# Attention of three of four batches: fp32 products on 64x64 tiles, and transposes on TensorE

## The chip, the cores and the metric

One core of one Trainium2 chip runs the whole program. The metric is the device time of one execution in microseconds (us), median of three runs.

## What is computed

Block-causal attention over 4 batches, 8 heads, 576 positions and 64 features per head, then two feed-forward layers on 2304 tokens of 512 features: 2048 hidden features with softplus, then 1536 with a gated SiLU behind an RMS norm.

```python
scores = scale * np.matmul(q, k.transpose(0, 1, 3, 2))
mask = block_i >= block_j              # blocks of 64 positions
attn = np.exp(scores - max); attn = attn / (sum + 1e-09)
x = np.matmul(attn, v)                 # then tokens x (heads * features)
h = x @ w_in; g = softplus(h); x = g @ w_out
xn = rms_norm(x) * rms_g
out = (silu(xn @ w_gate) * (xn @ w_val)) @ w_out
```

## The kernel before

**Order.** Every piece of work is registered with `op` (L82), with an engine, an estimated duration, a key (the wished time), and the tiles that it reads and writes. `Plan.schedule` (L145) then plays the whole program through with these estimates: on each engine it takes, among what is ready, the piece with the lowest key. `emit` (L271) does so up to 12 times with keys moved towards the latest possible times, and issues the instructions in the order of the best plan. The order on each engine is therefore fixed when the program is built; on the chip, an engine that waits for one instruction holds all behind it. `aop2`/`op2` (L424, L427) give pieces a choice of engines, and `schedule` picks by estimated end, with durations times `WEIGHT` (L74). PSUM has eight banks; `Banks` objects (L417) cap how many of them each kind of work may hold: feed-forward results `R_h`, attention `R_a` (scores and value products), transposes `R_tp`, and four accumulators `R_yp`.

**Feed-forward.** Tokens go in six blocks of 384 (`BLK`). Weights and activations are split into a high and a low fp32r part, and each product is three passes (`PASSES`). `g1` (L818) makes 128 hidden features with 12 matmuls of 384 columns, `g2` (L840) adds them into four accumulators with 12 more. The first phase runs 9 such steps for each of the six blocks, and attention of block j+1 is spread between the steps of block j; the second phase finishes the first layer, the third does the second layer (`g34`, L917, `g5`, L939). These two follow when attention is over.

**Attention.** A unit is one batch, one third of the query positions (`g`, 192 positions) and one pair of heads (`p`). It has three tiles `ib` of 64 positions; with two heads that is 128 rows, against n = 64 (3 g + ib + 1) keys. q lies block-diagonally, so that one matmul over 128 partitions gives both heads. `s_tile` (L594) makes the scores, takes the maximum on VectorE (L627), the exponential with the row sums on ScalarE (L661), and 1/sum (L669, L670). n = 576 goes in two halves of 288, as a bank holds 512 columns.

For batch 0 (`whole(u)`, L495; the first 12 units) the products are plain fp32, one matmul each, which the chip runs as two records; `s_turn` (L695) scales the probabilities, `turn` (L711) transposes them on TensorE in pieces of 128 columns, up to four a bank, and copies them out; `pv_whole` (L727) multiplies with v, for each head a matmul of 64 output rows, the two heads beside each other.

For batches 1 to 3, `prep_q`, `prep_k` and `prep_v` (L532 to L579) split q and k into two fp32r parts and v into two fp16 parts, the latter after scaling by a maximum that a small matmul (L561) spreads over the partitions. The scores are three passes of fp32r. `s_split` (L672) writes the probabilities as two fp16 halves, high (L681 to L683) and low (L686), and one DMA for each unit transposes them (L693). `pv` (L755) multiplies with v in three fp16 passes.

All matmuls but the transposes are issued at L422 (`mm`). `attention` (L789) registers the tiles in order; the value product of a unit follows its last tile by `LAG_T` = 6 tiles.

Of the kernel before, what the change touches and what calls it, by code (L numbers as in the profile page):

```python
# [68 lines left out]
class Plan:  # L69
# [4 lines left out]
    WEIGHT = {"ACT": 1, "DVE": 1, "POOL": 1}  # L74
# [7 lines left out]
    def op(self, eng, dur, key, fn, reads=(), writes=(), done=0.0, nbytes=0, after=(), alt=(), cols=0.0, port=False):  # L82
# [13 lines left out]
        for c in list(reads) + list(writes):  # L96
            b = c[0] if isinstance(c, tuple) else c
            if isinstance(b, Buf):
                if b.first is None:
                    b.first = i  # L100
                    if isinstance(b.ring, Banks):
                        self.takes[i] = b
# [42 lines left out]
    def schedule(self, key):  # L145
# [31 lines left out]
        for b in self.takes.values():  # L177
            b.ring.free = [0.0] * b.ring.cap
            for u in b.users:
                bank_of.setdefault(u, []).append(b)  # L180
            bank_left[b] = [len(b.users), 0.0]

        def at(i):
            t = max(free[eng[i]], ready_at[i])
            if i in self.takes:
                t = max(t, min(bank_free), min(self.takes[i].ring.free, default=INF))
            return t

        for _ in range(n):
# [16 lines left out]
            if i in self.takes:  # L206
                b = self.takes[i]
# [88 lines left out]
def t_mm(n):  # L296
    return max(0.11, (n + 32) / 2400)
# [46 lines left out]
def kernel(  # L344
# [12 lines left out]
    nc = tc.nc  # L357
# [59 lines left out]
    R_h, R_a, R_a0 = Banks(banks, 5), Banks(banks, 3), Banks(banks, 4)  # L417
# [58 lines left out]
    NQF = 2  # L476
    qf = [kp.tile([128, NG, 128], FP32, name=f"qf{i}") for i in range(NQF)]
    qbd = [kp.tile([128, 2, NG, 128], F32R, name=f"qbd{i}") for i in range(2)]
    R_raw = Ring(ap_, 3, [128, KT * 128], FP32, "raw")
    R_am = Ring(ap_, 2, [128, 3], FP32, "am")  # L480
# [5 lines left out]
    PITCH = [2, 6, 8]  # L486
    units = [(b, g, p) for b in range(B) for g in range(NG) for p in range(NP)]
    if 1:
        units[:2 * NP] = [(0, g, p) for p in range(NP) for g in range(2)]
    x_b, raw = {}, {}  # L490
# [4 lines left out]
    def whole(u):  # L495
        return u < 12

    def load_k(b, p, key):
        t = raw["k", b, p] = R_raw.new()
        att_ops.append(load(key, lambda: t()[:, 0:S], kT[b, p], writes=[t], nbytes=294912))  # L500

    k_y = R_y.new()
    k_raw = [R_raw.new() for p in range(2, NP)]
    k0 = lambda p: k_y().rearrange("p a c -> p (a c)")[:, S * p:S * p + S] if p < 2 else k_raw[p - 2]()[:, 0:S]
    k_cell = lambda p: (k_y, p) if p < 2 else k_raw[p - 2]

    def load_k0(p, key):
        att_ops.append(load(key, lambda: k0(p), kT[0, p], writes=[k_cell(p)], nbytes=294912))

    v_pst = [R_pst.new() for _ in range(NP // 2)]  # L510
    v0 = lambda p: v_pst[p // 2]().rearrange("p j c -> p (j c)").bitcast(FP32)[:, 640 * (p % 2):640 * (p % 2) + 640].rearrange("p (a c) -> p a c", c=128)

    def q_slot(u):
        i = u % (4 if whole(u) else 2)
        if i < 2:
            return ("qf", i), lambda: qf[i]
        t = v_pst[i - 2]
        return (t, "q"), lambda: t().rearrange("p j c -> p (j c)").bitcast(FP32)[:, 1280:1664].rearrange("p (i c) -> p i c", i=NG)

    def load_q(u, key):  # L520
        b, g, p = units[u]
        cell, t = q_slot(u)
        att_ops.append(load(key, t, qP[b, g, p], writes=[cell], nbytes=196608, dur=0.63))

    def load_v0(p, key):
# [645 lines left out]
```

## Time and profile before

| | us |
|---|---|
| median of 3 runs | 1055.45 (1055.14 to 1056.12) |
| profiled execution | 1055.07 |
| its span, first to last instruction | 1053.0 |
| TensorE busy | 1015.6 (96%) |
| VectorE busy | 710.2 (67%) |
| ScalarE busy | 529.4 (50%) |
| GpSimd busy | 163.9 (16%) |

The table is from the first part of the profile's page. "Busy" is the time in which at least one instruction's record is open. A matmul's record is longer than the time after which the next one can start, so that the distance from one start to the next is the better measure of what a matmul costs. Times in a stretch or a row are from the span's start.

### The profile page before, as it was taken

Reading aid. Unit: us, or ns where it says so; the run is one execution under the profiler, and the core shown is the slowest. Engines: PE = TensorE matmul, PEld = TensorE weight load, DVE = VectorE, ACT = ScalarE, POOL = GpSimd, SP = SyncE. Lnnn points to the kernel's source line nnn. Section 1 sums busy time; section 2 is a strip of 40 time slices with the busy share of each in tenths; the row PEclk is TensorE's granted clock in tenths of the full one; section 3 lists DMA queues with packets and bytes.
Section 4 is the critical chain, followed back from the end, with each engine's and each line's share of the span. In section 5 each row is a group of like instructions: output and inputs, shape, how many; then the busy total and the mean of one; then the engine's idle time right before and its main releaser. Section 6 shows DMA issues by size and latency. Waiting matters only on the chain.

```text
span 1053.0 us, 16902 instructions
## 1 busy us (share of the span) xinstructions
PE 1015.6 (96%) x6136; PEld 944.8 (90%) x6136; DVE 710.2 (67%) x1763; ACT 529.4 (50%) x1245; POOL 163.9 (16%) x225
## 2 busy tenths in 40 slices
PE   6798799999999999999999999999999999999998
PEld 4486689899999999999999999999999999999997
DVE  7989999999989967788879999522422422322222
ACT  6786787685767656777767563211211211211211
POOL 2333211211131003322333333000000000000000
PEclk8999899999999999999999999999999999999999
DMA  7444595785856453654544544300100100000000
GB/s 255 141 165 138 169 220 113 172 220 110 204 133 138 89 116 105 214 192 169 216 165 161 187 136 130 98 1 1 60 1 2 61 1 1 31 1 1 31 1 31
DMA packets 111635, 115.19 MB, mean 109 GB/s; under 512 B 84544, under 2 KB 92352, under 8 KB 110528
## 3 DMA queue, kind: packets, MB, share of 16 engines
q1 hardware_dynamic: 110976, 107.83, 36.3%
q0 software_dynamic: 576, 6.29, 1.6%
q8 instruction: 48, 0.79, 0.3%
q14 instruction: 35, 0.29, 0.1%
HBM read 72.03 MB, written 21.63 MB: 89 GB/s over the span
## 4 chain that ended last, share of the span: by engine, by line
PE 56%; DVE 4%; DMA 3%; ACT 1%; issue 1%; POOL 0%; ACTq 0%; DVEq 0%; POOLq 0%; SPq 0%
PE b L422 56%; DMA pt<-pst 1%; DMA wraw<-in_w2gv_dram 1%; DMA wraw<-in_w_dram 1%; DVE wa L456 0%; DVE g L337 0%; DVE r L891 0%; POOL wa L461 0%; DVE t L836 0%; ACT t L834 0%; DVE y L913 0%; DVE wa L458 0%; DVE y L884 0%; ACT wa L448 0%; ACT t L833 0%
## 5 line engine op out<-in xcount | busy, mean ns | idle before, releaser
L422 PE MATMUL b<-x,w 128*128 128x384 f32 x2880 | 546.1, 339 | 0.2 <-DVE x L753 0.2
L422 PEld LDWEIGHTS b<-x,w 128*128 128x128 f32 x2880 | 505.1, 188 | 11.7 <-issue 1.6
L422 PE MATMUL b<-g,w 128*128 128x384 f32 x1152 | 228.3, 341 | 3.6 <-DVE g L337 2.0
L422 PEld LDWEIGHTS b<-g,w 128*128 128x128 f32 x1152 | 200.9, 189 | 7.9 <-DVE g L337 3.4
L422 PE MATMUL b<-w,g 128*128 128x512 f32 x648 | 160.8, 393 | 0.0
L932 DVE TENSOR_TENSOR t<-b,t 128x384 f32<-128x384 f32 x72 | 39.9, 556 | 165.1 <-ACT t L931 165.1
L422 PEld LDWEIGHTS b<-w,g 128*128 128x128 f32 x648 | 120.6, 188 | 21.7
L461 POOL TENSOR_TENSOR wa<-wa,wraw 128x512 int32<-128x512 int32 x68 | 95.6, 1407 | 214.7 <-DVE wa L456 122.0
L931 ACT ACTIVATE t<-b 128x384 f32<-128x384 f32 x72 | 35.2, 491 | 175.5 <-PE b L422 175.5
L934 ACT CAST g<-t 128x384 fp32r<-128x384 f32 x72 | 36.9, 513 | 147.0 <-DVE t L933 147.0
L661 ACT ACTIVATE P<-b,nm 128x288 f32<-128x288 f32 (+8 forms) x160 | 79.4, 499 | 37.7 <-DVE nm L627 14.2
L933 DVE TENSOR_TENSOR t<-b,t 128x384 f32<-128x384 f32 x72 | 40.0, 556 | 62.3 <-PE b L422 62.3
L627 DVE TENSOR_REDUCE nm<-b 128x1 f32<-128x288 f32 (+8 forms) x160 | 70.0, 446 | 8.4 <-PE b L422 8.0
L422 PE MATMUL b<-khl,qbd 128*128 128x448 f32 (+7 forms) x360 | 69.4, 314 | 5.6 <-ACT P L661 3.3
L686 DVE SCALAR_TENSOR_TENSOR pst<-P,nm,pst 128x128 f16<-128x128 f32 (+4 forms) x108 | 67.7, 635 | 1.8 <-POOL pst L681 1.2
L422 PEld LDWEIGHTS b<-khl,qbd 128*128 128x128 f32 x360 | 57.1, 189 | 9.9 <-ACT P L661 4.8
L448 ACT ACTIVATE wa<-wraw 128x512 f32<-128x512 f32 x68 | 45.7, 673 | 35.6 <-DMA wraw<-in_w_dram 20.2
L327 ACT CAST g<-t 128x384 fp32r<-128x384 f32 x96 | 48.6, 511 | 29.5 <-DVE t L836 23.9
L935 DVE TENSOR_TENSOR g<-t,g 128x384 fp32r<-128x384 f32 x72 | 40.0, 556 | 34.3 <-ACT g L934 34.3
L836 DVE SCALAR_TENSOR_TENSOR t<-b,t 128x384 f32<-128x384 f32 x96 | 52.3, 550 | 15.7 <-ACT t L835 15.7
L337 DVE TENSOR_TENSOR g<-t,g 128x384 fp32r<-128x384 f32 x96 | 56.6, 595 | 8.7 <-ACT g L327 8.2
L833 ACT ACTIVATE t<-b 128x384 f32<-128x384 f32 x96 | 46.5, 487 | 25.6 <-PE b L422 25.2
(91 smaller groups left out, 1007.5 us busy)
## 6 DMA issues: line engine op xcount, KB each, us to landing
wraw<-in_w_dram SPq DMA_DIRECT2D x32, 512.0 KB, 3.7
wraw<-in_w2gv_dram SPq DMA_DIRECT2D x24, 512.0 KB, 3.7
yd<-y SPq DMA_DIRECT2D x12, 768.0 KB, 3.6
y<-yd SPq DMA_DIRECT2D x12, 768.0 KB, 4.4
qf<-in_qP_dram SPq DMA_DIRECT2D x42, 192.0 KB, 3.1
xd<-x SPq DMA_DIRECT2D x4, 1536.0 KB, 7.0
x<-xd POOLq DMA_DIRECT2D x4, 1536.0 KB, 7.2
wraw<-in_w2o_dram SPq DMA_DIRECT2D x12, 512.0 KB, 3.6
```

The costliest lines, as they stand in the source:

```text
L327: "ACT": ("ACT", t_act(n), lambda: nc.scalar.copy(dst(), src())),
L337: "DVE": ("DVE", t_dve(n), lambda: nc.vector.tensor_tensor(dst(), a(), b(), ALU.subtract)),
L422: nc.tensor.matmul(o, lhsT=l, rhs=r, start=start, stop=stop)
L448: op("ACT", t_act(CW), prio, lambda a=a, hv=halves: nc.scalar.activation(a(), hv()[1].bitcast(FP32), ACTF.Abs), [raw], [a])
L461: op("POOL", t_pool2(CW), prio, lambda a=a, hv=halves: nc.gpsimd.tensor_tensor(a().bitcast(I32), a().bitcast(I32), hv()[0].bitcast(I32), A ...
L627: aop("DVE", t_dve(cn), key, lambda sp=sp, col=col, cn=cn: nc.vector.tensor_reduce(nm()[:, col:col + 1], sp()[:, :cn], axis=AX.X, op=ALU.m ...
L661: aop("ACT", 0.24 + cn * 0.836e-3, key, lambda sp=sp, col=col, c0=c0, cn=cn: nc.scalar.activation(P()[:, c0:c0 + cn], sp()[:, :cn], ACTF.E ...
L686: aop("DVE", t_dve(c, True), key, lambda: nc.vector.scalar_tensor_tensor(lo(), pc(), r(), hi(), ALU.mult, ALU.subtract), [P, (P, "pad"), ( ...
L833: op("ACT", t_act(BLK, False), key - 5, lambda: nc.scalar.activation(e(), h()[:, :BLK], ACTF.Abs), [h], [e])
L836: op("DVE", t_dve(BLK), key - 5, lambda: nc.vector.scalar_tensor_tensor(e(), h()[:, :BLK], 0.0, e(), ALU.max, ALU.add), [h, e], [e])
L933: op("DVE", t_dve(BLK), key + 4, lambda: nc.vector.tensor_tensor(u(), va()[:, :BLK], u(), ALU.mult), [va, u], [u])
L935: op("DVE", t_dve(BLK), key + 4, lambda: nc.vector.tensor_tensor(g()[:, 1], u(), g()[:, 0].bitcast(FP32), ALU.subtract), [u, (g, 0)], [(g, ...
```

## The change

Batches 1 to 3 also use fp32 as given; the splits, the scaling of v and the transposing DMA go. A unit there has two pairs of heads (w for pairs 2w and 2w+1). Batch 0 keeps its steps, with new buffers. All k and v tiles have rings of six, q one of three; q of a double unit comes as two loads of 64 partitions each.

```diff
-    WEIGHT = {"ACT": 1, "DVE": 1, "POOL": 1}
+    WEIGHT = {"ACT": 1, "DVE": 2, "POOL": 1}
...
-    R_h, R_a, R_a0 = Banks(banks, 5), Banks(banks, 3), Banks(banks, 4)
+    R_h, R_a, R_a0 = Banks(banks, 4), Banks(banks, 4), Banks(banks, 4)
...
-    khl = [kp.tile([128, 2, S], F32R, name=f"khl{p}") for p in range(NP)]
-    vhl = [kp.tile([128, 2, KT, 128], FP16, name=f"vhl{p}") for p in range(NP)]
-    dsc = [kp.tile([128, 1], FP32, name=f"dsc{p}") for p in range(NP)]
...
-    qbd = [kp.tile([128, 2, NG, 128], F32R, name=f"qbd{i}") for i in range(2)]
...
-    R_P = Ring(ap_, 3, [128, KT * 128], FP32, "P")
-    R_nm = Ring(ap_, 2, [128, 16], FP32, "nm")
-    R_pst = Ring(ap_, 2, [128, 26, 128], FP16, "pst")
-    R_pt = Ring(ap_, 2, [128, 26, 128], FP16, "pt")
...
+    R_k = Ring(ap_, 6, [128, S], FP32, "k")
+    R_v = Ring(ap_, 6, [128, KT, 128], FP32, "v")
+    R_q = Ring(ap_, 3, [128, NG, 128], FP32, "q")
+    R_P = Ring(ap_, 4, [128, KT * 128], FP32, "P")
+    R_nm = Ring(ap_, 3, [128, 32], FP32, "nm")
+    R_pt = Ring(ap_, 4, [128, 13, 128], FP32, "pt")
...
+    units = [(0, g, p) for p in range(NP) for g in range(2)] + [(0, NG - 1, p) for p in range(NP)]
+    units += [(b, g, w) for b in range(1, B) for g in range(NG) for w in range(NP // 2)]
...
+        t = k_next[p] = R_k.new()
+        att_ops.append(load(key, t, kT[b, p], writes=[t], nbytes=294912))
+
+    def load_v(b, p, key):
+        t = v_next[p] = R_v.new()
+        att_ops.append(load(key, t, vP[b, p], writes=[t], nbytes=327680))
...
+            h = slice(64 * a, 64 * a + 64)
+            att_ops.append(load(key, lambda h=h: t().rearrange("p b (i c) -> p b i c", i=2)[h], qP[b, g, 2 * p:2 * p + 2, h, :, h].rearrange("i q b c -> q b i c"), writes=[(t, a)], nbytes=196608, dur=0.63))
+
```

`s_pair` is new, for batches 1 to 3. `product` issues four matmuls of 64 partitions by 64 output rows: head `a` chooses the partitions and the bank, pair `i` the output rows.

```diff
+    def s_pair(u, ib, key, after):
+        b, g, w = units[u]
+        n = 64 * (NG * g + ib + 1)
+        chunks = [(0, n)] if n <= 512 else [(0, n // 2), (n // 2, n // 2)]
+        if ib == 0:
+            pts[u], part[u] = [R_pt.new() for a in range(2)], R_nm.new()
+        nm, q, ks = part[u], q_b[u], [k_b[2 * w + i] for i in range(2)]
...
+
+        def product(heads, c):
+            c0, cn = chunks[c]
+            for a in heads:
+                sp[a, c] = ring_a(u).new()
+            parts = [(a, slice(64 * a, 64 * a + 64), i, slice(64 * i, 64 * i + 64)) for a in heads for i in range(2)]
+
+            def qk():
+                for a, h, i, o in parts:
+                    mm(sp[a, c]()[o, :cn], q()[h, ib, o], ks[i]()[h, c0:c0 + cn], True, True)
+
+            rd = [(q, a) for a in heads] + ks
+            if c == 0 and heads[0] == 0:
+                qk_op.append(len(plan.ops))
+            aop("PE", 0.02 + cn * 1.667e-3, key, qk, rd, [sp[a, c] for a in heads], after=after, cols=t_mm16(4 * cn))
+
+        for c in range(len(chunks)):
+            product(range(2), c)
```

Then follow the maxima of each head, the exponentials, 1/sum, the scaling of the probabilities and `turn`, as in batch 0, for each of the two heads; the small operations on maxima and sums take both heads at once. `s_split` goes; `turn` and the value product are those of batch 0, the latter once for each pair `i`:

```diff
-        aop2([alts[e] for e in ("POOL", "DVE", "ACT")], key, [P, (P, "pad"), (nm, "r", ib)], [(pst, ib, 0)])
-        aop("DVE", t_dve(c, True), key, lambda: nc.vector.scalar_tensor_tensor(lo(), pc(), r(), hi(), ALU.mult, ALU.subtract), [P, (P, "pad"), (nm, "r", ib), (pst, ib, 0)], [(pst, ib, 1)], port=True)
...
-            att_ops.append(op("SP", 1.175, key, lambda: nc.sync.dma_start_transpose(out=pt()[:, c0:c1, :], in_=pst().rearrange("p j c -> p (j c)")[:, 128 * c0:128 * c1]), rd, [(pt, i) for i in range(f, ib + 1)], done=1.0, nbytes=(c1 - c0) * 40960))
...
+        for a in range(2):
+            P = part[u, ib, a]
...
+            aop2([alts[e] for e in ("POOL", "ACT", "DVE")], key, [P, (nm, "r", ib)], [P])
+            for j0 in range(0, nj, 4):
+                turn(g, ib, P, pts[u][a], j0, min(4, nj - j0), key)
...
+    def turn(g, ib, P, pt, j0, nj, key):
+        o = R_tp.new()
 
         def prod():
             for j in range(nj):
                 nc.tensor.transpose(o()[:, 128 * j:128 * j + 128], P()[:, 128 * (j0 + j):128 * (j0 + j) + 128], ones)
...
+    def pv(u, i, key):
+        b, g, w = units[u]
+        pt, o, pitch = pts[u], ring_a(u).new(), 2 + g
+        p = w if whole(u) else 2 * w + i
+        v = v_b[p]
...
+
+        def keys(j, h, i0):
+            t, c = (pt[0], h) if whole(u) else (pt[h], i)
+            return t()[:, slice(i0 * pitch + j, (NG - 1) * pitch + j + 1, pitch), 64 * c:64 * c + 64]
...
                 for h in range(2):
                     mm(
                         o()[64 * h:64 * h + 64, 64 * i0:GQ],
-                        v0(p)[0:kk, j, 64 * h:64 * h + 64],
-                        pf()[0:kk, slice(i0 * pitch + j, (NG - 1) * pitch + j + 1, pitch), 64 * h:64 * h + 64],
+                        v()[0:kk, j, 64 * h:64 * h + 64],
+                        keys(j, h, i0)[0:kk],
                         j == 0,
                         j == nj - 1,
                     )
...
+    share = [1 if whole(u) else 2 for u, ib in tiles]
     LAG_T = 6
+    pv_at = [[] for t in range(nt + LAG_T)]
+    for u in range(len(units)):
+        t, need = NG * u + NG - 1, LAG_T
+        while need > 0 and t < nt + LAG_T - 1:
+            t += 1
+            need -= share[t] if t < nt else 2
+        pv_at[t].append(u)
...
+                b, g, w = units[u]
+                (s_tile if whole(u) else s_pair)(u, ib, when(t), after(t))
+                if ib == NG - 1 and u + R_q.bufs < len(units):
+                    load_q(u + R_q.bufs, when(t) - 5)
...
+            for u in pv_at[t]:
+                b, g, w = units[u]
+                for i in range(1 if whole(u) else 2):
+                    pv(u, i, when(t - 1) + -1)
+                pts.pop(u)
```

The planner's estimates change as well: a double tile counts as two in dividing attention into six parts, and feed-forward matmuls count 2.5 ns + 0.4459 ns per column.

## Rows read from the trace of the kernel before

**Rows 1.** Stretches: us, busy us of PE, PEld, DVE, ACT, POOL, granted clock, DMA share, GB/s.

```profile
0.00:35.00 35.00, 22.10 (x115) 14.83 (x116) 27.32 (x107) 22.11 (x66) 10.35 (x27) 0.90 0.66 229
35.00:60.00 25.00, 19.54 (x114) 12.92 (x113) 24.09 (x82) 18.12 (x52) 7.79 (x11) 1.00 0.50 169
60.00:98.00 38.00, 35.17 (x213) 29.34 (x211) 34.79 (x100) 28.78 (x70) 12.15 (x18) 1.00 0.45 136
98.00:125.00 27.00, 22.29 (x144) 17.70 (x142) 24.86 (x89) 19.92 (x50) 6.56 (x12) 0.87 0.52 155
125.00:400.00 275.00, 268.44 (x2066) 252.95 (x2067) 249.22 (x742) 192.48 (x516) 45.54 (x102) 0.99 0.66 151
400.00:1053.00 653.00, 648.08 (x3493) 617.03 (x3491) 349.89 (x647) 248.01 (x497) 81.50 (x59) 1.00 0.23 80
```

**Rows 2.** Matmul groups, 125 to 400 us: count; busy, mean ns; idle before, releasers.

```profile
L422 PE MATMUL b<-x,w 128*128 128x384 f32 x516 | 105.4, 340 | 0.0
L422 PE MATMUL b<-g,w 128*128 128x384 f32 x496 | 102.5, 343 | 0.2 <-DVE g L337 0.2
L422 PE MATMUL b<-khl,qbd 128*128 128x448 f32 (+7 forms) x330 | 64.0, 316 | 3.6 <-ACT P L661 2.3 <-DVE t L836 1.3
L422 PE MATMUL b<-pt,vhl 128*64 128x192 f16 (+2 forms) x708 | 32.8, 236 | 3.4 <-DMA pt<-pst 2.9 <-ACT P L661 0.4
L422 PE MATMUL b<-ones,am 128*128 128x128 f32 x16 | 3.3, 286 | 0.0
```

**Rows 3.** The chain that ended last: start, length, what; a run of first-layer matmuls.

```profile
439.37 101.18 PE b L422 x577
```

**Rows 4.** Timeline, TensorE, 208 to 226 us: start, length, matmul groups.

```profile
215.34 0.42 PE L422 MATMUL b<-khl,qbd 128*128 128x64 f32 x3
215.59 0.77 PE L422 MATMUL b<-g,w 128*128 128x384 f32 x3
...
219.13 0.47 PE L422 MATMUL b<-khl,qbd 128*128 128x192 f32 x3
219.44 0.70 PE L422 MATMUL b<-g,w 128*128 128x384 f32 x3
...
223.54 0.68 PE L422 MATMUL b<-khl,qbd 128*128 128x384 f32 x3
224.06 0.68 PE L422 MATMUL b<-g,w 128*128 128x384 f32 x3
```

**Rows 5.** Timeline, TensorE, 47 to 55 us, batch 0.

```profile
47.98 0.52 PE L716 MATMUL b<-ones,P 128*128 128x128 f32 x3 [0.20 <-DVE P L704]
48.25 0.77 PE L422 MATMUL b<-x,w 128*128 128x384 f32 x3
48.86 1.02 PE L422 MATMUL b<-y,qf 128*128 128x512 f32 x2
...
53.73 1.09 PE L422 MATMUL b<-pt,pst 128*64 128x192 f32 x12
54.75 1.02 PE L422 MATMUL b<-y,qf 128*128 128x448 f32 x2
```

**Rows 6.** Timeline, TensorE, 252 to 256 us.

```profile
252.78 1.22 PE L422 MATMUL b<-g,w 128*128 128x384 f32 x6
253.93 0.85 PE L422 MATMUL b<-pt,vhl 128*64 128x192 f16 x18
254.71 0.79 PE L422 MATMUL b<-g,w 128*128 128x384 f32 x3
255.34 0.85 PE L422 MATMUL b<-x,w 128*128 128x384 f32 x4
```

**Rows 7.** Groups of the whole span, costliest first.

```profile
L661 ACT ACTIVATE P<-b,nm 128x288 f32<-128x288 f32 (+8 forms) x160 | 79.4, 499 | 37.7 <-DVE nm L627 14.2 <-DVE nm L639 10.3 <-DVE nm L669 4.7
...
L686 DVE SCALAR_TENSOR_TENSOR pst<-P,nm,pst 128x128 f16<-128x128 f32 (+4 forms) x108 | 67.7, 635 | 1.8 <-POOL pst L681 1.2 <-ACT pst L683 0.2
...
L716 PE MATMUL b<-ones,P 128*128 128x128 f32 x100 | 18.9, 296 | 12.8 <-DVE P L704 6.7 <-ACT P L705 3.6 <-DVE nm L639 1.2
```

More of the change, by code (lines that the diff above doesn't have):

```diff
@@ L101, in op @@
                     if isinstance(b.ring, Banks):
-                        self.takes[i] = b
+                        self.takes.setdefault(i, []).append(b)
                     if b.older is not None:
@@ L176, in schedule @@
         bank_of, bank_left = {}, {}
-        for b in self.takes.values():
+        for b in (b for bs in self.takes.values() for b in bs):
             b.ring.free = [0.0] * b.ring.cap
@@ L205, in schedule @@
             i = pick[1]
-            if i in self.takes:
-                b = self.takes[i]
+            for b in self.takes.get(i, ()):
                 bank[b] = bank_free.index(min(bank_free))
@@ L495, in whole @@
     def whole(u):
-        return u < 12
+        return u < NW
+    k_b, v_b, k_next, v_next = {}, {}, {}, {}
     def load_k(b, p, key):
[L499 to L518, printed above, removed]
+        t = k_next[p] = R_k.new()
@@ L597, in s_tile @@
         chunks = [(0, n)] if n <= 512 else [(0, n // 2), (n // 2, n // 2)]
-        d = qbd[u % 2]
         if ib == 0:
-            pts[u], part[u] = R_pt.new(), (R_nm.new(), [])
-            if not whole(u):
-                psts[u] = R_pst.new()
-        nm, done = part[u]
-        qr = [("qbd", u % 2, l) for l in range(2)]
-        kr = [("khl", p, 0), ("khl", p, 1)]
-        if whole(u):
-            kt, k = k_cell(p), lambda: k0(p)
-            (qc, qt), kr = q_slot(u), [kt]
-            qr = [qc]
+            pts[u], part[u] = [R_pt.new()], R_nm.new()
+        nm = part[u]
+        k, q = k_b[p], q_b[u]
         bank = []
@@ L711, in turn @@
-    def turn(u, ib, j0, nj, key):
-        g, P, pt, o = units[u][1], part[u, ib], pts[u], R_tp.new()
+        for a in range(2):
+            P = part[u, ib, a]
+            alts = {
+                "POOL": ("POOL", t_pool(n), lambda P=P, a=a: nc.gpsimd.tensor_scalar(P()[:, :n], P()[:, :n], one(24, a), 1.0, ALU.mult, ALU.mult)),
+                "DVE": ("DVE", t_dve2(n) + 0.06, lambda P=P, a=a: nc.vector.tensor_scalar(P()[:, :n], P()[:, :n], one(24, a), None, ALU.mult)),
+                "ACT": ("ACT", t_act(n) + 0.09, lambda P=P, a=a: nc.scalar.activation(P()[:, :n], P()[:, :n], ACTF.Copy, scale=one(24, a))),
+            }
+            aop2([alts[e] for e in ("POOL", "ACT", "DVE")], key, [P, (nm, "r", ib)], [P])
+            for j0 in range(0, nj, 4):
+                turn(g, ib, P, pts[u][a], j0, min(4, nj - j0), key)
@@ L965, in cost @@
         n = 64 * (NG * units[u][1] + ib + 1)
-        return 3 * t_mm(n if n <= 512 else n // 2) * (1 if n <= 512 else 2) + 0.13 * ((n + 127) // 128)
-    per_block = len(tiles) // NB
+        return n * 1.667e-3 + share[t] * 0.25 * ((n + 127) // 128)
+    blk = [next((t for t in range(nt) if sum(share[:t]) >= sum(share) * j // NB), nt) for j in range(NB + 1)]
     step = 24 * t_mm(BLK)
     T0 = 36
-    attn_pe = [sum(cost(t) for t in range(per_block * j, per_block * (j + 1))) for j in range(NB)] + [0.0]
+    attn_pe = [sum(cost(t) for t in range(blk[j], blk[j + 1])) for j in range(NB)] + [0.0]
     win = [T0]
@@ L978 @@
         acc = 0.0
-        for t in range(per_block * j, per_block * (j + 1)):
+        for t in range(blk[j], blk[j + 1]):
             when_.append(a + (b - a) * acc / attn_pe[j])
```

277 lines of the change are left out of this document (74 added, 203 removed).

## The prediction

> **What bounds the kernel now.** The totals of the page say little, since the kernel has stages, so I read the table of stretches first [rows 1]. From 400 us on, attention is over and TensorE is busy for 648.1 of 653.0 us: nothing of the change touches that stretch, and it stays as it is. Up to 400 us attention runs between the feed-forward products, and two engines are near their end at once: from 125 to 400 us TensorE is busy for 268.4 and VectorE for 249.2 of 275 us. Before 125 us VectorE is the fuller one (24.1 of 25, 34.8 of 38, 24.9 of 27) and TensorE idles for 12.9 + 5.5 + 2.8 + 4.7 = 25.9 us [rows 1].
>
> The question is thus which of the two ends last between 125 and 400 us. A record of a matmul outlasts the slot that it takes (340 ns mean for 384 columns, where 577 of them in a row took 101.18 us, 175 ns each) [rows 2, 3], so "busy" hides short waits. I counted the work instead: 516 + 496 feed-forward matmuls at 175 ns are 177.4 us; the 330 of 360 score matmuls are 46.7 (of 50.9, below); the 708 of 720 value matmuls are 35.6 (of 24.0 plus 36 switches of 0.34, below); 16 small ones at 0.11 are 1.8 [rows 2]. That is 261.5 of 275 us, so true waits are about 13 us, of which the profile names 3.4 before the value products (2.9 on the transposing DMA) and 3.6 before the score products [rows 2]. TensorE is the bound there, with VectorE just behind. A change that takes work from VectorE can give back at most those waits; what it adds to TensorE counts in full.
>
> **The change, part by part, as TensorE time.** All of it concerns batches 1 to 3: 12 (batch, pair) sets, each with nine query tiles of n = 64, 128, ... 576 keys, 2880 columns in all.
>
> *Score products removed.* Three passes each. In the stretch from 208 to 226 us a score product sits between feed-forward ones, and the distance to the next start is its price: 0.25 us at n=64, 0.31 at 192, 0.52 at 384 [rows 4]. Interpolated (0.28, 0.38, 0.45, then 0.07 more per 64 columns, and 0.80 for the two halves of n=576) a set costs 0.25+0.28+0.31+0.38+0.45+0.52+0.59+0.66+0.80 = 4.24 us, times 12 is 50.9.
>
> *Score products added.* Four 64x64 tiles (two heads by two pairs) in fp32. The price per column comes from batch 0, which is fp32 already: a value product of 12 records, two heads side by side, takes 53.73 to 54.75, 1.02 us [rows 5]. These are six pairs, 4x192 + 2x128 = 1024 columns; less 0.15 for leaving the layout that is 0.85 ns per column and pass, two cycles at 2.4 GHz (0.833), and two passes make 1.667 ns. One after the other the 12 records would need 1.7 us, so two column tiles do run at once. No row shows two row tiles at once. Lower bound, all four at once: 6 double sets x 2880 columns x 1.667 ns = 28.8 us; upper bound, two and two: 57.6. I take the lower, as the nearest row (the two column tiles) shows full overlap.
>
> The Trainium skill, "TensorEngine Tiling (Array Packing)", section Tiling Modes, lists 64x64 as four independent tiles that can multiply in parallel; by it the columns would be the 28.8 us.
>
> *The switch of layout.* At 252.78 six g·w matmuls start, at 253.93 a value product of 18 records, at 254.71 three g·w, at 255.34 x·w [rows 6]. From 252.78 to 255.34 are 2.56 us. Nine matmuls at 175 ns are 1.58, the 18 records (nine pairs, 1536 columns at 0.417 ns) 0.64: 0.34 us are left over, 0.10 ahead, 0.14 inside and at its end, 0.10 in the next operation. So going from whole-array matmuls to half-width tiles and back costs 0.34 us. The value products pay it already; the score products start to pay it now, since feed-forward products surround each of them [rows 4]: 54 tiles, six with two column halves, so 60 x 0.34 = 20.4 us. Lower bound 54 x 0.23 = 12.4 (the late next weight load falls into a wait), upper 60 x 0.44, with one more late load of 0.1. Score products after: 28.8 + 20.4 = 49.2, against 50.9: a wash.
>
> *Value products.* Columns per set 256 + 512 + 832 = 1600, 19,200 in all. Before three fp16 passes, 19,200 x 1.25 ns = 24.0 us; after two fp32 passes, 19,200 x 1.667 = 32.0. +8.0. Both pairs of a unit now come ready together; adjacent, they share a switch. Between 0 and 18 x 0.34 = 6.1 us; I take 3 as won, because the planner may put other matmuls between them.
>
> *Transposes on TensorE.* Each probability tile is turned in pieces of 128 columns: 25 per set, 300 in all, in 120 groups. In batch 0 three of them take 47.98 to 48.25, and the three x·w behind them 48.25 to 48.86, 0.61 instead of 0.53 [rows 5]. 0.35 us for three, 0.12 each: 300 x 0.12 = +36.0 us. Bounds 0.09 and 0.15: 27 to 45. All of it is new: the DMA did it before, beside everything.
>
> *Removed besides.* The matmuls that spread a maximum of v over the partitions: 24 records, of which 16 were busy for 3.3 us [rows 2], and their slots are somewhat shorter: -3.
>
> Sum on TensorE: -50.9 + 49.2 + 8.0 - 3 + 36.0 - 3 = +36.3 us.
>
> **What comes back as waits.** VectorE loses the low halves of the probabilities, 67.7 us [rows 7], a share of the high halves, and all preparation of q, k and v. It takes on part of copying the turned tiles out of PSUM (300 x 128 columns) and of the scaling; the planner now counts its time double and so leans to ScalarE and GpSimd, which are at 192.5 and 45.5 of 275 us [rows 1]. So VectorE stops being tight. The transposing DMA and its 2.9 us of waits go [rows 2]. Between 98 and 125 us, where batch 1 was prepared, TensorE idles for 4.7 us and its clock was granted at 0.87 [rows 1]. Lower bound nothing; upper bound all 13 us of 125 to 400 and all 25.9 idle before it, 39. What is late next: the chain of batch 0, unchanged, and PSUM banks (below). I take 4 of the 13, 8 of the 13.0 idle between 35 and 125, 2 of the first 12.9 (more buffers) and 1 for the clock: -15.
>
> *A wait that is new.* A transpose waits on TensorE for the scaled probabilities, and behind it in the engine's order stand feed-forward matmuls, for whose results ScalarE and VectorE wait. In batch 0 the 40 groups stood idle for 12.8 us [rows 7], 0.32 each, but there TensorE had little else to do. Lower bound nothing, upper 120 x 0.32 = 38; I take nothing beyond the 9 us of waits that I leave after 125 us, since feed-forward work can be put ahead of a group that isn't ready. That work is the cover.
>
> *SP's queue* loses 36 transposing DMAs and has as many q loads as before (two for each of 18 units), in shorter pieces. They are asked for three units ahead, so I cost them at nothing; the units between are the cover, and without it a load of some 3 us would show at each of 18 units.
>
> Forecast: 1053.0 + 36.3 - 15 = 1074 us span. The profiled run took 1055.07, 2.1 more than its span, and the median is 1055.45, so the two stand for each other: 1076 us.
>
> **The rivals.**
>
> *Banks (1095).* A pair tile takes two of the eight PSUM banks at once, and at n=576 four; four hold the accumulators of the second product. Before, a tile held one (or two) for a maximum and an exponential, the latter 499 ns in the mean [rows 7]; now two banks for twice that, while 120 groups of transposes need banks as well. For it: the profile already names waits of score matmuls on the exponential that frees a bank, 2.3 us [rows 2]. Against it: VectorE and ScalarE get faster through the chain. Price: 54 tiles that wait some 0.3 us each, 15 us, in place of 4 gained: 1095.
>
> *Row tiles don't overlap (1105).* The change then doesn't do what it says: +28.8 us. Against it only the neighbour, the column tiles.
>
> *The clock (1120).* The granted clock was 0.87 from 98 to 125 us, where TensorE waited most, and 1.00 from 35 to 98, where transposes of batch 0 were densest [rows 1], so transposes don't bring it down by themselves. If the whole stage ran at 0.87, 295 us would become some 44 longer.
> The Trainium skill, "TensorE: Matmul & The Clock Gate", Part 4, says that the full clock does not engage for transposes; by that rule this rival decides. The trace of batch 0 speaks against it, at 1.00.
>
> *Faster: VectorE paces the stage (1043).* VectorE is 92 to 96% busy between 35 and 125 us [rows 1]. If it is what holds TensorE up everywhere until 400 us, all 39 us of waits go instead of 15, which is 1052; and if the switches then fall into gaps that remain, paired value products save 3 more and 60 late weight loads 0.1 each: 1043. It decides from the point at which over 36 us of waits vanish. Against it: the count above finds only 13 us of waits after 125 us.
>
> **How the numbers follow.** Forecast 0.55, banks 0.18, row tiles 0.10, clock 0.05, faster 0.12. A measurement of this kernel tells about 0.2%, 2 us, from no change. Slower by more: 0.55 + 0.18 + 0.10 + 0.05 less a tail of 0.02 = 0.86; faster 0.09 and same 0.05 share the last case and that tail. The range goes from 1057, where switches and waits take their good ends, to 1106, which takes in banks and row tiles; the last rival and the clock, 0.17, stay out.
>
> **What would show it.** Feed-forward matmuls at 175 ns, as now. Score products: four records within some 20 ns, twice a product; a start-to-next-start of 0.83 us at n=288 with the switch; if 1.3, the row tiles run in turn. Transposes: 300 more of 0.12 us. VectorE far below 249 us between 125 and 400, TensorE's time there longer by some 30, the end of attention at about 420 us. Fewer than 5 us of idle from 98 to 125. I would be wrong if score products stand back to back (no switch between them), or if idle time before 125 us falls by much more than 10.

## The result, and the profile after

The changed kernel took 1066.15 us (median of 4 runs, 1065.32 to 1069.38), the kernel before 1055.78 us beside it (1055.14 to 1056.96): ratio 1.0103, 95% interval 1.0079 to 1.0126, slower by 10.4 us in the medians and 10.9 by the ratio. The forecast was 1076 us, +20.5: the sign is right, the time lies within the range of 1057 to 1106, and the loss was put about twice too high. The profiled execution is the longest of the four: 1069.38 us, span 1067.5.

The table of stretches of the kernel after, in the columns of [rows 1]:

```profile
0.00:35.00 35.00, 26.61 (x145) 19.81 (x145) 25.12 (x109) 27.04 (x85) 14.37 (x33) 0.90 0.74 256
35.00:60.00 25.00, 21.50 (x124) 16.12 (x124) 22.28 (x67) 23.33 (x61) 15.20 (x21) 0.97 0.63 206
60.00:98.00 38.00, 35.94 (x210) 31.11 (x209) 28.32 (x72) 29.87 (x68) 14.35 (x20) 0.93 0.44 134
98.00:125.00 27.00, 23.59 (x199) 17.02 (x198) 21.74 (x66) 22.12 (x73) 10.68 (x20) 1.00 0.53 166
125.00:400.00 275.00, 271.65 (x2051) 221.93 (x2051) 127.69 (x386) 203.16 (x554) 29.14 (x95) 1.00 0.16 53
400.00:1067.50 667.50, 663.45 (x3571) 631.90 (x3569) 359.54 (x623) 275.05 (x554) 96.79 (x71) 1.00 0.24 79
```

Against [rows 1], VectorE falls from 249.2 to 127.7 us between 125 and 400 us, and the DMA share from 0.66 to 0.16: the low halves and the transposing DMAs are gone. TensorE rises from 268.4 to 271.7, and its idle time before 125 us falls from 25.9 to 8.4 + 3.5 + 2.1 + 3.4 = 17.4, over half of it, 12.9 to 8.4, in the first 35 us. ScalarE is now the second engine (203 of 275), not near its end.

TensorE's groups between 125 and 400 us, in the columns of [rows 2]:

```profile
L423 PE MATMUL b<-x,w 128*128 128x384 f32 x463 | 96.3, 346 | 0.0
L423 PE MATMUL b<-g,w 128*128 128x384 f32 x432 | 92.7, 349 | 0.0
L634 PE MATMUL b<-ones,P 128*128 128x128 f32 x284 | 44.5, 276 | 2.4 <-ACT P L623 2.4
L423 PE MATMUL b<-pt,v 128*64 128x192 f32 (+2 forms) x464 | 39.5, 309 | 1.0 <-ACT P L611 0.6 <-ACT pt L640 0.2
L423 PE MATMUL b<-k,q 64*64 64x288 f32 (+8 forms) x408 | 37.9, 441 | 0.0
```

284 transposes (L634) are new there, and the same 275 us hold only 463 + 432 = 895 feed-forward matmuls instead of 1012. The score products (`k,q`, 64x64) never stood idle, where those before waited 3.6 us [rows 2]; the transposes waited 2.4 us for scaled probabilities (L623).

TensorE's timeline of the kernel after, two places (start, length, group):

```profile
146.63 2.27 PE L423 MATMUL b<-x,w 128*128 128x384 f32 x12
148.83 1.09 PE L423 MATMUL b<-k,q 64*64 64x512 f32 x8
149.85 0.79 PE L423 MATMUL b<-g,w 128*128 128x384 f32 x3
150.48 0.60 PE L634 MATMUL b<-ones,P 128*128 128x128 f32 x4
150.84 0.42 PE L423 MATMUL b<-g,w 128*128 128x384 f32 x1
...
170.75 2.62 PE L423 MATMUL b<-g,w 128*128 128x384 f32 x14
173.30 1.96 PE L423 MATMUL b<-pt,v 128*64 128x192 f32 x24
175.19 0.98 PE L423 MATMUL b<-k,q 64*64 64x448 f32 x8
```

From 146.63 to 150.48 are 3.85 us. Fifteen feed-forward matmuls at 175 ns are 2.625, and 512 columns at 1.667 ns 0.853: 0.37 us are left over, the switch. The eight records start in two fours, 148.830, .836, .843, .850 and 149.310 to .330: all four tiles run at once. Four transposes start 0.11 us apart; the g·w behind them starts 0.03 us after the last, but the next one only at 151.10, 0.26 us later instead of 0.175, so the four take 0.44 us. At 173.30 a value product stands ahead of a score product, and the two share a switch.

**A budget for TensorE.** The experiments are read with one count: each matmul at its shortest slot (some 173 ns per 384 columns of feed-forward; 1.667 ns per column for fp32, over the tiles that run at once; 0.109 us per transpose, and as the least for a narrow whole-array score record); the switches to half-width tiles and back, counted in the order of the records, at 0.345 us (the 0.34 of the prediction and the 0.37 above); changes between 128x64 and 64x64 tiles (row changes) at 0.15 us. At the 175 ns of the prediction the work of every kernel would be some 10 us more and its waits as much less; the differences between kernels stay.

The starts in the kernel after bear out both prices: 30 times a score product stands alone between feed-forward matmuls with no idle time, and there 0.36 to 0.44 us are left over, 0.37 in the median; where a value and a score product stand beside each other with one row change, 0.52 to 0.55 are.

What the span has beyond these I call waits. They hold all idle time, lower clocks and whatever the prices miss. "To 125" and "then" divide at 125 us and at the end of attention, after which 10 to 14 us remain in every kernel. A negative second column is a kernel faster than before.

| kernel | against before, us | work | switches | row changes | waits to 50 / to 125 / then / after attention | sum of waits |
|---|---|---|---|---|---|---|
| before | 0 | 971.1 | 48 | 16 | 25.7 / 15.6 / 10.6 / 11.0 | 62.9 |
| after | +10.9 | 985.2 | 82 | 32 | 16.7 / 14.5 / 6.0 / 11.9 | 49.1 |
| e1, whole-array scores | +23.2 | 1015.8 | 48 | 16 | 16.9 / 9.2 / 2.2 / 12.3 | 40.6 |
| e2, half the transposes | -7.4 | 968.9 | 82 | 31 | 22.1 / 7.6 / 5.5 / 11.3 | 46.5 |
| e3, VectorE work back, planned | +17.3 | 985.2 | 79 | 33 | 19.5 / 10.5 / 12.4 / 11.5 | 53.9 |
| e4, layout held | +13.6 | 985.2 | 60 | 39 | 22.8 / 8.3 / 11.9 / 12.4 | 55.5 |
| e5, before with VectorE x2 | -9.2 | 971.1 | 48 | 16 | 25.4 / 11.0 / 8.3 / 10.6 | 55.3 |
| e6, after with VectorE x1 | +16.8 | 985.2 | 80 | 29 | 21.0 / 15.0 / 9.7 / 10.9 | 56.6 |
| e7, three buffers | +19.9 | 985.2 | 87 | 29 | 21.4 / 10.2 / 12.2 / 11.9 | 55.7 |
| e8, more switches | +17.1 | 985.2 | 102 | 20 | 18.4 / 10.9 / 6.2 / 12.1 | 47.6 |
| e9, before with VectorE x3 | -7.1 | 971.1 | 48 | 16 | 21.4 / 17.3 / 9.6 / 9.9 | 58.2 |
| e10, six buffers | +12.4 | 985.2 | 81 | 33 | 19.1 / 13.5 / 5.4 / 13.9 | 51.9 |
| e11, after with VectorE x3 | +10.9 | 985.2 | 82 | 30 | 17.4 / 11.5 / 5.9 / 12.7 | 47.5 |
| e12, VectorE work back, same order | +31.4 | 985.2 | 82 | 32 | 16.0 / 17.4 / 21.1 / 12.7 | 67.2 |

The second column is the ratio to the kernel before, run beside it, times 1056 us; its 95% intervals are 2 to 4 us to either side. The other columns are of one profiled execution each, and the granted clock differs among them: that of after shows 0.93 from 60 to 98 us, above, where e1 shows 1.00, which is part of its 14.5. The profile records the stretches at a granted clock of 0.50, the level of 1.2 GHz: 17.1 us in all before (all in the first 131 us), 13.7 after (in the first 90 us), none in e1, 3.4 in e8, 10.2 in e5, 17.1 in e6 and in e12. From 58.7 to 62.1 us after, one of them, feed-forward matmuls start 0.32 us apart. What the lower level cost is estimated as the price of the matmuls issued there: 7.4 us before, 6.8 after, 0 in e1, 1.7 in e8, 4.5 in e5, 7.1 in e6, 8.2 in e12, 10.6 in e9. It is a part of the waits.

So the change adds 14.1 us of work, 34 switches (11.7) and 16 row changes (2.4): 28.2 us. With +10.9 by the ratio, 17.3 us of waits must have gone (13.8 in the profiled execution). The clock can explain the difference of the two: the profiled execution after had a mean granted clock of 0.994 and took 1069.4 us, the other three had 0.998 to 0.999 and took 1065.3 to 1066.8. The experiments ask whether the 28.2 is priced rightly, and what took the waits away.

### The profile page after: what moved, and what is told of

It reads as the page before. It is cut to its first block, busy times and chain, and to the rows that moved or that the text cites. A ratio compares the mean times of both kernels' runs of the same rounds, so it can differ in the third digit from the quotient of the medians.

```text
span 1067.5 us, 16853 instructions
## 1 busy us (share of the span) xinstructions
PE 1042.7 (98%) x6292; PEld 937.9 (88%) x6292; DVE 584.7 (55%) x1318; ACT 580.6 (54%) x1386; POOL 180.5 (17%) x259
## 4 chain that ended last, share of the span: by engine, by line
PE 82%; DVE 6%; ACT 5%; DMA 3%; issue 2%; POOL 1%; SPq 0%; POOLq 0%; ACTq 0%; DVEq 0%
PE b L423 78%; PE b L634 4%; DMA wraw<-in_w_dram 2%; POOL wa L462 1%; DVE wa L459 1%; DVE wa L457 1%; DVE g L338 1%; DVE wa L453 1%; DMA wraw<-in_w2gv_dram 1%; ACT wa L449 1%; ACT t L733 1%; ACT t L734 1%; ACT w L328 0%; DVE t L736 0%; ACT P L611 0%
## 5 line engine op out<-in xcount | busy, mean ns | idle before, releaser
L423 PE MATMUL b<-g,w 128*128 128x384 f32 x1152 | 233.3, 345 | 0.8 <-DVE t L736 0.7
L423 PEld LDWEIGHTS b<-g,w 128*128 128x128 f32 x1152 | 200.3, 189 | 14.6 <-issue 10.1
L423 PE MATMUL b<-k,q 64*64 64x288 f32 (+14 forms) x560 | 71.6, 435 | 7.3 <-DMA q<-in_qP_dram 4.2
L634 PE MATMUL b<-ones,P 128*128 128x128 f32 x400 | 66.1, 280 | 10.0 <-ACT P L564 2.8
L611 ACT ACTIVATE P<-b,nm 128x288 f32<-128x288 f32 (+8 forms) x120 | 60.1, 504 | 21.6 <-DVE nm L604 19.0
L599 DVE TENSOR_REDUCE nm<-b 128x1 f32<-128x288 f32 (+8 forms) x120 | 49.9, 452 | 39.7 <-PE b L423 39.2
L634 PEld LDWEIGHTS b<-ones,P 128*128 128x128 f32 x400 | 48.6, 142 | 25.8 <-issue 5.0
L338 DVE TENSOR_TENSOR g<-t,g 128x384 fp32r<-128x384 f32 x96 | 58.7, 613 | 22.0 <-ACT g L328 21.3
L835 DVE TENSOR_TENSOR g<-t,g 128x384 fp32r<-128x384 f32 x72 | 42.2, 587 | 35.2 <-ACT g L834 35.2
L640 ACT COPY pt<-b 128x512 f32<-128x512 f32 (+3 forms) x125 | 53.2, 443 | 15.0 <-PE b L634 14.0
```

What stands on the lines that cost most here:

```text
L338: "DVE": ("DVE", t_dve(n), lambda: nc.vector.tensor_tensor(dst(), a(), b(), ALU.subtract)),
L423: nc.tensor.matmul(o, lhsT=l, rhs=r, start=start, stop=stop)
L599: aop("DVE", t_dve(cn), key, lambda o=sp[a, c], col=col, cn=cn: nc.vector.tensor_reduce(nm()[:, col:col + 1], o()[:, :cn], axis=AX.X, op=A ...
L611: aop("ACT", 0.24 + cn * 0.836e-3, key, lambda P=P, o=sp[a, c], col=col, a=a, c0=c0, cn=cn: nc.scalar.activation(P()[:, c0:c0 + cn], o()[: ...
L634: nc.tensor.transpose(o()[:, 128 * j:128 * j + 128], P()[:, 128 * (j0 + j):128 * (j0 + j) + 128], ones)
L640: "ACT": ("ACT", t_act(c, False), lambda: nc.scalar.copy(d(), o()[:, :c])),
```

## The experiments

Theory T, on which the forecast rests: TensorE's sum sets the time, and waits go because work leaves VectorE. Rivals: switches or transposes fall into gaps; PSUM banks make new waits; the waits went for another reason, such as the factor with which the planner counts VectorE's time, the additional buffers, or the order of the work.

**e1: the scores as whole-array products again**, fp32, block-diagonal q, one pair at a time, in all batches as in batch 0. This takes the 64x64 tiles of the scores away and leaves the transposes; the sharing out of attention over its six parts is fitted to the smaller units.

```diff
-    units += [(b, g, w) for b in range(1, B) for g in range(NG) for w in range(NP // 2)]
+    units += [(b, g, p) for b in range(1, B) for g in range(NG) for p in range(NP)]
...
-        return u < NW
+        return True
...
```

> Batches 1 to 3 keep fp32, but the scores of each pair are one block-diagonal product over the whole array, as in batch 0, instead of four 64x64 tiles; one pair a unit, one bank a tile. TensorE then switches layout 48 times instead of 82. Theory 'TensorE's sum' (columns, switches of 0.35 us and transposes all count in full): columns 57.6 instead of 28.8 us, 34 switches less are -12, 16 changes of row layout less are -2: about +15 us against the changed kernel, 1081 us. Theory 'switches are hidden in waits': +29, 1095 us. Theory 'banks' (a pair tile's two or four banks make TensorE wait): less than +10, below 1076 us.

1079.54 us (1077.98 to 1082.19), ratio 1.0220 (1.0197 to 1.0244): 12.3 us above after. The sum says +30.6 of columns, -34 x 0.345 and -16 x 0.15, +16.5. The group of the score products between 125 and 400 us, with two passes over twice the columns:

```profile
L423 PE MATMUL b<-k,q 128*128 128x448 f32 (+7 forms) x204 | 66.4, 427 | 0.0
```

TensorE is busy for the whole 275 us in this stretch and the waits after 125 us are down to 2.2: the difference of some 4 us to the sum lies in the waits. In the profiled executions they are 8.5 us lower than after, and some 6.8 of that are the clock, which e1 never lost. In these two kernels the tiles are worth their switches; no score product stood idle, so there is no sign of a wait for banks in either.

**e2: half of the transposes.** Only head 0's probabilities are turned, and head 1's value product reads head 0's, so head 1's part of the result isn't attention any more. The copies of the transposes that are left out, on VectorE and ScalarE, go too.

```diff
-            pts[u], part[u] = [R_pt.new() for a in range(2)], R_nm.new()
+            pts[u], part[u] = [R_pt.new()] * 2, R_nm.new()
...
-                turn(g, ib, P, pts[u][a], j0, min(4, nj - j0), key)
+                if a == 0:
+                    turn(g, ib, P, pts[u][a], j0, min(4, nj - j0), key)
```

> The changed kernel, in which only the first head's probabilities of each pair tile are transposed and copied; the second head's value product reads the first head's. 150 of 400 transposes and 60 of 160 groups are left out, with their copies. Theory 'TensorE's sum': 150 x 0.11 to 0.12 us = 17 to 18 us less, 1048 us. Theory 'VectorE and ScalarE pace the stage': their copies fall by about 25 us, TensorE's gain shows only in part: less than 10 us, above 1056.

1048.96 us (1048.33 to 1050.24), ratio 0.9930 (0.9913 to 0.9947): 18.3 us below after for 150 transposes, 0.122 us each. By the budget 16.3 of it are the transposes' slots, and some 2 are waits, in which the copies may have a part. Without that half the changed kernel is faster than before. The transposes count in full; nothing hides them.

**e3: VectorE's work back.** Needless operations of the size of the removed low halves, for 108 tiles, which nothing waits for (120 in the trace, busy for 70.6 us).

```diff
+    scr = kp.tile([128, 512], FP32, name="scr")
+    scl = kp.tile([128, 512], FP16, name="scl")
...
         for a in range(2):
+            for c in ((nj * 128,) if nj < 5 else (320, 320)):
+                aop("DVE", t_dve(c, True), key, lambda a=a, c=c: nc.vector.scalar_tensor_tensor(scl[:, :c], scr[:, :c], one(24, a), scr[:, :c], ALU.mult, ALU.subtract), ["scr", (nm, "r", ib)], ["scl"], port=True)
```

> The changed kernel with VectorE given back as much time as the removed low halves took: 108 tiles' worth of the same operation on a scratch tile, some 68 us, which nothing waits for. Theory 'TensorE's sum': VectorE stands at 128 of 275 us between 125 and 400 us and has room; 0 to +4 us, 1066 to 1070. Theory 'the waits that came back were VectorE's': a good part of the 14 us of waits that went returns, +8 to +14, 1074 to 1080.

1073.46 us (1073.14 to 1074.65), ratio 1.0164 (1.0144 to 1.0184): 6.4 us above after, a little under what the theory of VectorE's relief expected and well over TensorE's sum alone. The planner saw the work, though, and ordered everything anew, so load and order are mixed here; e6, e7 and e8, below, moved by 6 to 9 us with another order and no added work. e12 parts them.

**e4: the layout held.** The planner prefers, among the ready TensorE operations, one that needs no switch, with a bonus of 8 us on its due time.

```diff
+    SWITCH, HOLD = 0.34, 8.0
...
-                pick = min(r for r in ready[e] if at(r[1]) <= t)
+                pick = min((r for r in ready[e] if at(r[1]) <= t), key=lambda r: (r[0] + ((r[1] in self.tiled) != mode) * self.HOLD, r[1]))
...
```

> The changed kernel, its planner made to keep TensorE in one layout: an operation of the other layout is taken only when its key is 8 us ahead, and the estimate counts a switch. 60 switches instead of 82, 39 changes of row layout instead of 32. Theory 'TensorE's sum': -22 x 0.35 + 7 x 0.15 = -6.7 us, 1059. Theory 'switches are hidden in waits': no change, 1066. If holding operations back makes new waits: slower than 1066.

1070.17 us (1069.33 to 1070.83), ratio 1.0129 (1.0112 to 1.0145): not 6.5 us below after, as 22 switches less and 7 row changes more would be, but 2.7 above. The waits of TensorE between 125 and 400 us (us in total, times, longest):

```profile
PE b L430 <- ACT P L618: 2.6, 2, 1.6
PE b L641 <- ACT pt L647: 1.3, 2, 0.8
PE b L641 <- DVE nm L610: 0.5, 1, 0.5
```

A reading of these lines that was not tested: a product that is held back frees its banks and its buffers later (L618 is the exponential, L647 the copy of turned probabilities out of PSUM), and TensorE then waits for the engines behind it. Waits after 125 us doubled, 6.0 to 11.9, of which the profile names only a part as idle time (3.4 to 5.3 us up to 400 us); before that their sum stayed (31.2 and 31.1). The expectation's third case came true.

**e8: the opposite, a layout left as soon as possible** (the same edit with HOLD = -8.0).

> The changed kernel with its planner made to leave a layout as soon as it can: 102 switches and 20 changes of row layout instead of 82 and 32, with the same products. If a switch costs what the starts show, 0.345 us, and a change of rows 0.15: 20 x 0.345 - 12 x 0.15 = +5.1, 1071 us. If switches fall beside other waits: 1065 to 1067. If the changed order makes waits of its own, as holding the layout back did: above 1074.

1073.92 us (1071.12 to 1074.88), ratio 1.0162 (1.0139 to 1.0186): 6.2 us above after, where the two prices say 5.1, and the sum of waits is within 2 us of after's. That agrees with a switch that isn't hidden, but it doesn't show its price by itself: e8 lost some 5 us less to the clock than after in the profiled executions, so its other waits are some 3.6 us higher, and e6 and e7 moved by as much with 2 switches fewer and 5 more. The price rests on the starts.

**e5 and e6: the planner's factor alone.** The change also makes the planner count VectorE's time double; that is one line, independent of the rest. It was put into the kernel before, and taken out of the kernel after:

```diff
-    WEIGHT = {"ACT": 1, "DVE": 1, "POOL": 1}
+    WEIGHT = {"ACT": 1, "DVE": 2, "POOL": 1}
```

> The kernel before with one figure changed: its planner counts VectorE's time double, as the changed kernel's does. All work stays, split scores, low halves and transposing DMAs too; TensorE's sum is that of before (48 switches). Two theories of the some 15 us of waits that the change gave back, 9 of them in the first 50 us. W, the weight: in before TensorE waits 5.5 us there for probabilities that VectorE scales, and in the changed kernel ScalarE scales them; then this kernel runs at 1045 to 1050 us. R, relief: it is the removed work (low halves, preparation of q, k and v) that freed VectorE; then 1054 to 1058, as before. If ScalarE becomes late instead, above 1058.

> The changed kernel with its planner counting VectorE's time once, as before. TensorE's sum is 1 us shorter by its order (80 switches instead of 82, 29 changes of row layout instead of 32). W, the weight made the gain of the first 50 us: 1072 to 1077 us. R, the removed work made it: 1063 to 1068.

e5: 1047.20 us (1046.63 to 1047.74), ratio 0.9913 (0.9898 to 0.9927): the kernel before, with one figure changed, is 9.2 us faster, and beats both kernels. e6: 1074.21 us (1069.02 to 1075.57), ratio 1.0159 (1.0131 to 1.0187), 5.9 us above after. A part of both can be the clock: e6's one execution at a mean clock of 0.997 took 1069.0 us, its three at 0.992 to 0.993 took 1074.1 to 1075.6. What the factor moves is seen in VectorE's groups of the first 125 us; before, and then e5:

```profile
L337 DVE TENSOR_TENSOR w<-wa,w 128x512 fp32r<-128x512 f32 x18 | 12.2, 679 | 0.0
L704 DVE TENSOR_SCALAR P<-P,nm 128x64 f32<-128x64 f32 (+8 forms) x27 | 11.9, 445 | 0.3
...
L328 DVE CAST w<-wa 128x512 fp32r<-128x512 f32 x18 | 7.5, 415 | 0.7 <-POOL wa L461 0.7
```

```profile
L337 DVE TENSOR_TENSOR w<-wa,w 128x512 fp32r<-128x512 f32 x9 | 6.1, 683 | 0.0
...
L328 DVE CAST w<-wa 128x512 fp32r<-128x512 f32 x1 | 0.4, 408 | 0.0
```

In e5 VectorE scales no probabilities of batch 0 any more (L704, 27 before) and makes 10 of the pieces of weights instead of 36; after has 2 of the former (L563). The size fits theory W, but not the place that I had expected. In the first 50 us e5 stood idle ahead of the transposes as long as before; its group there:

```profile
L716 PE MATMUL b<-ones,P 128*128 128x128 f32 x52 | 11.6, 322 | 11.0 <-ACT P L705 7.7 <-POOL P L703 2.7 <-issue 0.5
```

and that of before:

```profile
L716 PE MATMUL b<-ones,P 128*128 128x128 f32 x48 | 10.8, 317 | 11.4 <-DVE P L704 5.5 <-ACT P L705 3.6 <-DVE nm L639 1.2
```

The name changed from VectorE to ScalarE, the wait did not. The gain came behind: waits from 50 to 125 us 15.6 to 11.0, and then 10.6 to 8.3.

**e9 and e11: the factor three**, in the kernel before and in the kernel after.

> The kernel before with VectorE's time counted three times by its planner; counted twice it took 1047.2 us. If VectorE's own queue is what TensorE waits for until 400 us, there is more to give back: 1040 to 1046. If work has moved to ScalarE and GpSimd as far as it pays (in the kernel with the factor two, TensorE's waits are already on probabilities that ScalarE scales, 8.5 us, and GpSimd, 2.7): 1046 to 1053. If those two are now overloaded: above 1053.

> The changed kernel with VectorE's time counted three times; counted once it took 1074.2 us and twice 1066.2. 82 switches and 30 changes of row layout, so TensorE's sum stays. VectorE is busy for 128 of 275 us from 125 us on already, so only the start can gain: 1063 to 1067; above 1069 if ScalarE, busy for 203 of 275 us there, becomes late.

e9: 1050.07 us (1046.53 to 1052.57), ratio 0.9933 (0.9905 to 0.9961). e11: 1067.92 us (1067.60 to 1068.49), ratio 1.0103 (1.0081 to 1.0126). Neither gains over the factor two. So the change at equal factors costs +16.8 (one), +10.9 + 9.2 = +20.1 (two) and +10.9 + 7.1 = +18.0 us (three). Of the kernels made from after that do its work in another order (e4, e6, e7, e8, e10, e11), none ran faster than it, so some of its low figure may be the luck of one order; no run settles that.

**e7 and e10: buffers for probabilities.** The change has four instead of three (`R_P`); tried with three and with six.

```diff
-    R_P = Ring(ap_, 4, [128, KT * 128], FP32, "P")
+    R_P = Ring(ap_, 3, [128, KT * 128], FP32, "P")
```

> The changed kernel with three buffers for probabilities instead of four, as many as before the change. The planner's order then has 87 switches and 29 changes of row layout, which is 1.3 us more by 0.345 and 0.15 us each. If the fourth buffer is what gave waits back (a score product can run ahead of the turned probabilities): 1072 us or more. If not: 1066 to 1069.

> The changed kernel with six buffers for probabilities instead of four; three cost 10.7 us. The planner's order then has 81 switches and 33 changes of row layout, so TensorE's sum stays. Buffers theory (a pair tile that can't have its two buffers holds up the chain that TensorE waits for): two more pairs ahead bring some of the waits that are left, 1058 to 1063. Order theory (the fourth buffer gave no slack, the planner's order of three was only a worse one): 1064 to 1069.

Three: 1076.86 us (1073.89 to 1077.68), ratio 1.0188 (1.0169 to 1.0208), 9.0 above after. Six: 1070.96 us (1066.27 to 1071.78), ratio 1.0117 (1.0082 to 1.0152), no gain over four. Two pairs of buffers are needed and more than that bring nothing, or three is only a worse order: these two runs don't tell which, since each number of buffers gives another order.

**e12: e3 with the order kept.** The same VectorE work, issued behind the reciprocals and unknown to the planner (120 operations in the trace again, 66.7 us).

```diff
...
-        aop("DVE", 0.08, key, lambda: nc.vector.reciprocal(two(24), two(16)), [(nm, "t", ib)], [(nm, "r", ib)])
+        def recip():
...
+            nc.vector.reciprocal(two(24), two(16))
+            for a in range(2):
+                for c in ((nj * 128,) if nj < 5 else (320, 320)):
+                    nc.vector.scalar_tensor_tensor(scl[:, :c], scr[:, :c], 0.5, scr[:, :c], ALU.mult, ALU.subtract)
+
+        aop("DVE", 0.08, key, recip, [(nm, "t", ib)], [(nm, "r", ib)])
```

> The changed kernel with the same 68 us of needless VectorE work in batches 1 to 3 as the run that returned it before, but issued behind the reciprocals and not counted by the planner, so that every engine keeps the changed kernel's order (82 switches, 32 changes of row layout). The earlier run let the planner see the work, which also changed the order; its waits after 125 us doubled, 6.0 to 12.4 us. If the load itself made TensorE wait: again some 1.016 of the kernel before, 1072 to 1076 us. If the changed order did: 1.010 to 1.012, 1066 to 1069 us.

1087.78 us (1082.87 to 1089.74), ratio 1.0297 (1.0271 to 1.0322): 20.5 us above after, more than either theory expected. So the load does make TensorE wait, and in e3, where the planner placed the work and ordered the rest around it, some 14 of that were avoided. The stretch from 125 to 400 us and TensorE's longest wait from there to 420 us:

```profile
125.00:400.00 275.00, 265.92 (x1948) 211.51 (x1944) 174.77 (x481) 194.03 (x529) 34.28 (x95) 0.99 0.15 50
```

```profile
PE b L423 <- DVE x L688: 5.1, 5, 1.9
```

VectorE is busy for 174.8 of 275 us, 64%, and yet TensorE's waits after 125 us rise from 6.0 to 21.1. The largest that the profile names is on L688, which writes `x`, the input of feed-forward matmuls. It points to this: what counts is not VectorE's share but that work stands ahead of an operation that a product is planned for. About half of the rise is named as idle time in the profile.

## Why the prediction was right, and where its size was off

**The score products: "a wash" held.** The four tiles run at once, so the columns cost the lower bound of 28.8 us, and the rival of row tiles in turn (1105) is out. The Trainium skill, "TensorEngine Tiling (Array Packing)", section Tiling Modes, lists four independent tiles for 64x64. The starts 6 to 7 ns apart agree. The scores removed were 52.7 us by the budget, against 50.9.

**The switches: 60 were counted, 34 came.** This is a mis-sized term. I had put the score products' 60 switches at 20.4 us and let the value products share 3 us of theirs, 17.4 in all; the planner puts score and value products side by side far more often than that, as at 173.30 above, and 34 switches and 16 row changes are 14.1 us. The price per switch was right (0.37 in the timeline and in the median of 30 places; e8 agrees). The sign of being wrong that I named, score products back to back, came true in part: some stand beside value products, which is how 60 became 34.

**The transposes: right.** 36.0 forecast; e2 makes 300 x 0.122 = 36.6, its copies included, and the four at 150.48 take 0.11 each. The budget's shortest slot makes 32.7, the rest being in its waits.

The sum was thus forecast at +36.3, and the budget has +28.2: 3.3 from the switches, 3.3 from the transposes as the budget prices them, 1.8 from the scores, against 0.4 for the small matmuls.

**The waits: 15 forecast, some 17 gone, for partly another reason and in another place.** After 125 us I had let go 4 of 13; 4.6 went (10.6 to 6.0). Before it I had 10, and 1 more for the clock; 10.1 went by the budget (25.7 + 15.6 to 16.7 + 14.5), though not where I had put them: by the idle time in the stretches, 4.5 in the first 35 us, where I had 2, and 2.0 + 0.8 + 1.3 = 4.1 from there to 125, where I had 8. The size came near in part by luck. The step that failed is the cause: the prediction named the planner's factor in half a sentence and gave 12 of the 15 to the work that leaves VectorE and the transposing DMA, 2 to buffers and 1 to the clock. The factor alone was worth 9.2 us (e5; 7.1 at three, e9) on the kernel before and 5.9 on the kernel after (e6), with the clock's part in them not taken off, so the change proper gives back only some 8 to 11 of its 28. Of that part e12 shows that VectorE's load is able to make it: some 68 us of load cost 20.5 us in a fixed order, and 6.4 came with it in a new one. How the rest is divided among load, buffers and the other work of preparation stays open, since kernels with equal work differ by some 7 us in the waits of the first 50 us alone (16.0 to 22.8 in the table), and by as much after 125 us, by their order.

**The new wait of the transposes: nothing, as taken.** 2.4 us between 125 and 400 us, within the 9 left. **SP's queue: nothing.** No row of TensorE's groups above names a load.

**The banks rival (1095) is out**: the score products stood idle for 0.0 us. **The clock rival (1120) is out**: granted 1.00 (the level of 2.4 GHz) from 98 us on, with 284 transposes between 125 and 400 us. Before 98 us the lower level cost some 6.8 us, by the estimate above, against 7.4 before the change in its first 131 us. The prediction's reason, that TensorE waited most from 98 to 125 us, was misread: its idle share there was 4.7 of 27 us at 0.87, and 5.5 of 25 at 1.00 from 35 to 60 [rows 1]. The Trainium skill, "TensorE: Matmul & The Clock Gate", Part 4, says that the full clock doesn't engage for transposes; among feed-forward matmuls, as here, the trace speaks against it. **The faster rival (1043)** needed over 36 us of waits to vanish; some 17 did.

**The end of attention: 396.0 us, not "about 420".** That step was an error of reading: I added the forecast to 400 us, which is only the edge of a stretch. The last result of attention was written at 382.5 us before, so it moved by 13.5, nearly all of the span's 14.5.

## What to carry to other kernels

A change that brings a new setting of the planner along is two changes: put the setting alone into the old kernel first, since here it was worth 9 us there and hid about half of the loss. Read the granted clock of each execution before comparing waits: here the lower level cost from nothing (e1) to some 8 or 10 us (e12, e9) of them. Count layout switches in the order of the records, not one for each product: neighbours share them, and the price per switch (0.35 to 0.37 us here) is worth reading from the timeline, as is the price of holding back, since the kernel that held them back (e4) was slower with 22 switches fewer. An engine busy for 64% of the time held up a full one (e12), it seems because its work stood ahead of what the full one needed, so relief of it is worth asking for in microseconds of waits, not in its share.

## What the runs showed of the hardware that I had not expected

Four 64x64 fp32 products of 512 columns start within 20 ns of each other, in two fours 0.48 us apart: both passes of neighbouring tiles go side by side. Going between 128x64 and 64x64 tiles costs 0.15 to 0.18 us, an estimate from what two neighbouring products with one such change leave over (0.52 to 0.55 us) against one alone (0.37); that is less than the 0.37 us of going from whole-array products to tiles and back. An fp32 transpose of 128x128 takes 0.11 us in a group of four, and taking 150 of them away with their copies gave 0.122 us each.
